# The generator of an S4D kernel: row copies put later, a second PSUM bank for products, doubling factors in one three-bank tile

## The chip, the cores and the metric

The kernel runs on one core of a Trainium2 chip. The metric is the time of one execution on the device in microseconds, as a median over runs. A core has five engines with instruction queues of their own: TensorE (PE, whose weight loads are listed as PEld), VectorE (DVE), ScalarE (ACT), GpSimd (POOL) and SyncE (SP), which here only issues transfers. Engines wait for each other through semaphores.

## The reference

Two sublayers under adaptive layer norm work on a sequence of L = 2048 rows of D = 576 channels. The first is an S4D convolution: a kernel K of 2048 taps is generated for each channel from N = 128 complex modes and convolved causally with the input. The second is a dense feed-forward layer with ReLU and 4608 hidden units.

```python
# convolution
dt = jnp.exp(log_dt)
A = -jnp.exp(log_A_real) + 1j * A_imag
C = (C_real + 1j * C_imag) * dt[:, None]
P = jnp.exp((A * dt[:, None])[:, :, None] * pos[None, None, :])
K = 2.0 * jnp.einsum("dn,dnl->dl", C, P).real
Kf = jnp.fft.rfft(K, L2)
Uf = jnp.fft.rfft(u_t, L2)
y = jnp.fft.irfft(Uf * Kf[None, :, :], L2)[:, :, :L]
...
mod = (_silu(c) @ w_mod).reshape(c.shape[0], 6, 1, -1)
sa, ca, ga, sb, cb, gb = (mod[:, 0], mod[:, 1], mod[:, 2], mod[:, 3], mod[:, 4], mod[:, 5])
h = _layernorm(x, axis=-1) * (1 + ca) + sa
x = x + ga * conv(h)
h = _layernorm(x, axis=-1) * (1 + cb) + sb
x = x + gb * (jnp.maximum(h @ w1, 0) @ w2)
```

## The kernel before

The sequence is cut into four blocks of 512 rows. The convolution's kernel K is generated by the class `KGen` for block 0 first, in its method `first`, while nothing else can run; then `main` runs the convolution of block 0 (`conv(0)`, which starts with the layer norm of its rows x), and from there on the feed-forward layer, with the remaining blocks of K (`rest`) and the remaining convolutions woven between. The change lies in `first` and what it calls.

K at tap 32a + b of a channel is a sum over the modes, which lie on the 128 partitions, of a coarse factor W1 (16 values of a) and a fine factor W2 (32 values of b), both complex. A group g is 96 channels, as two halves u of H = 48; the six groups run in three pairs (`CHUNKS`: groups 0 and 1, 2 and 3, 4 and 5). The text calls them pair 0, 1 and 2. The program of a pair, as it is written:

- `raw(c)` makes the arguments of a pair: 22 "turns" k, each an ACT copy to integers and a DVE subtraction (L105, L115), and 38 exponentials E on ACT. For pair 1 and 2 this code is issued between the groups of the pair before.
- `values(g, then)` makes W2 of group g, first the odd half of its slots, then `then()`, then the even half (`half_values`). ACT takes sines s (into two PSUM banks) and cosines c of the turns; DVE makes the imaginary parts of W2 (L150, L151) and POOL the real ones (helper at L59). POOL also clears and copies one slot of each W2 (L163, L164). `start` makes the products tc (POOL) and Tc (DVE) that open W1. `powers` makes four doubling factors Zp in PSUM, and two more, zs, in SBUF: ACT's sines and cosines, then times E on DVE (L199) and on POOL. W2 and zs are stored to DRAM on SP.
- `make(g)` doubles W1 four times with the factors Zp (`doubling`: DVE multiplies t and T at L224 and L225 and adds at L227 and L228; in the last doubling POOL adds, "W<-T,T" in the profile), stores W1, and runs 384 matmuls on PE (`products`, L236) from W1 and W2 into one PSUM bank, kps. It returns `rows`, which copies kps to rows of K in SBUF on ACT (ke), and with every third group stores them (kd_0_0 and kd_0_1, L323) on SP.

In the loop of `first`, the first group's row copy of a pair stands right after its `make` and one step of the next `raw`; the second group's stands in `then` of the first group of the next pair, between its odd and even half.

ACT and POOL run in program order, as the helpers `act` and `pool` keep it. The order on DVE, PE and SP is set by the scheduler of the language from the program and its dependencies.

Of PSUM's eight banks the sines take two, the temporary T one, the factors Zp four (two tiles of two banks), and kps one. Beside this, `mod` works out three of the modulation vectors (ga, ca, sa) from w_mod on PE; their weights wm_ga, wm_ca, wm_sa are loaded into the first three of the five rotating buffers ("slots") of W2's tag, and their products go through the same bank as kps. One of those products is issued ahead of the values, one in `then` of group 0, one after pair 0's values. W2_n names half n = 2g + u.

With the pools of `KGen` closed, the pool of `conv(0)` lies over the same part of SBUF. Its tile cb of `mod_late` (L524, L525, 160 columns, a copy of ct on DVE) lies over one of W2's slots, and in DVE's queue stands ahead of the layer norm's statistics (BN_STATS, L692).

Of the kernel before, what the change touches and what calls it, by code (L numbers as in the profile page):

```python
# [10 lines left out]
F32 = mybir.dt.float32  # L11
# [7 lines left out]
P = 128  # L19
# [6 lines left out]
G = 96  # L26
# [14 lines left out]
def strips(t, k):  # L41

    w = t.shape[1] // k
    return bass.AP(tensor=t.tensor, offset=t.offset, ap=[[w, P], [P * w, k], [1, w]])


class KGen:
# [10 lines left out]
    def pool(self, out, a, b, op):  # L58
        self.tc.keep_in_program_order(self.nc.gpsimd.tensor_tensor(out, a, b, op=op))  # L59

    def open(self, ctx):

        pool = lambda n, **kw: ctx.enter_context(self.tc.tile_pool(name=n, bufs=1, **kw))
        self.pa, self.pc, self.pt, self.pw = (pool(f"kg_{x}") for x in "actw")
        self.ps, self.ph = pool("kg_ps", space=PSUM), pool("kg_ph", space=PSUM)

    def bank(self, name):
        return self.ph.tile([P, 512], F32, tag="ph", name=name)

    def setup(self, I):  # L70
        nc, pc = self.nc, self.pc
# [115 lines left out]
    def powers(self, g, e, f):  # L187

        v, p = self.nc.vector.tensor_tensor, self.pool
        Z = self.ps.tile([P, 2, 512], F32, tag="Z", bufs=2, name=f"Zp_{g}")[:, :, 0 : 4 * G]  # L190
        Z = Z.rearrange("p r (i c) -> p r i c", c=G)
        zs = self.pc.tile([P, 2, 2, G], F32, tag="zs", bufs=2, name=f"zs_{g}")
        c = self.abs(f)
        self.act(Z[:, 1], f[:, 0:4], AF.Sin, scale=-TWO_PI)
        self.act(zs[:, :, 1], f[:, 4:6], AF.Sin, scale=-TWO_PI)
        self.cos(Z[:, 0], c[:, 0:4])
        self.cos(zs[:, :, 0], c[:, 4:6])
        for r in (1, 0):
            v(Z[:, r], Z[:, r], e[:, 0:4], op=ALU.mult)  # L199
            p(zs[:, :, r], zs[:, :, r], e[:, 4:6], op=ALU.mult)  # L200
        self.Z[g] = Z, zs

    def doubling(self, g):

        v, p = self.nc.vector.tensor_tensor, self.pool
        W1, Z = self.W1[g], self.Z[g][0]
        flat = "p u a r c -> p u (a r) c"
# [22 lines left out]
    def products(self, ps, W1, W2, u):  # L230

        for q in range(12):
            for dd in range(4):
                ch = dd * 12 + q
                for r in range(2):
# [6 lines left out]
                    )  # L242

    def first(self, setup, mod):

        nc, k = self.nc, self.k
        self.W1, self.Z, W2s, EF, ke = {}, {}, {}, {}, {}

        def raw(c):
            w = slice(CHUNKS[c][0] * G, CHUNKS[c][1] * G)  # L250
            F, E = self.turns(w), [None] * 5
            for m in (2, 3, 0, 1, 4):
                E[m] = self.exps(w, m)
                if m in (3, 1):
                    yield
            for g in range(*CHUNKS[c]):
                gs = slice((g - CHUNKS[c][0]) * G, (g - CHUNKS[c][0]) * G + G)
                EF[g] = [e[:, :, gs] for e in E], [f[:, :, gs] for f in F]

        def values(g, then):  # L260
            E, F = EF.pop(g)
            W2 = W2s[g] = [
                self.pw.tile([P, 2, 32, H], F32, tag="W2", bufs=5, name=f"W2_{2 * g + u}")
                for u in range(2)
            ]
            self.half_values(g, W2, E[2:4], F[0], True)
            then()
            self.half_values(g, W2, E[0:2], F[1], False)
            for u in range(2):
                nc.sync.dma_start(  # L270
                    out=strips(k.W2d[2 * g + u], 4),
                    in_=W2[u].rearrange("p r (y b) c -> p (r y) (b c)", y=2),
                )
            self.powers(g, E[4], F[2])
            zs = self.Z[g][1]
            for u in range(2):
                nc.sync.dma_start(out=k.Zd[2 * g + u], in_=zs[:, :, :, u * H : u * H + H])

        def make(g):
            self.doubling(g)  # L280
            for u in range(2):
                nc.sync.dma_start(
                    out=strips(k.W1d[2 * g + u], 2),
                    in_=self.W1[g][:, u].rearrange("p (y a) r c -> p y (a r c)", y=2),
                )
            if g % 3 == 0:
                ke[0] = self.pc.tile([P, 16, 72], F32, tag="ke", bufs=1, name=f"ke_{g}")
            ps = self.bank(f"kps_{g}")[:, :384].rearrange("p (q a) -> p q a", a=16)
            for u in range(2):
                self.products(ps, self.W1[g], W2s[g][u], u)  # L290

            def rows():
                qs = slice(24 * (g % 3), 24 * (g % 3) + 24)
                self.act(ke[0][:, :, qs], ps.rearrange("p q a -> p a q"), AF.Copy)
                if g % 3 == 2:
                    self.store(0, g // 3, ke[0].rearrange("p a q -> p (a q)"), nc.sync)

            return rows

        next(mod)  # L300
        for _ in raw(0):
            pass
        next(mod)
        setup()
        rows = lambda: next(mod)
        for c, (a, b) in enumerate(CHUNKS):
            for g in range(a, b):
                values(g, rows if g == a else lambda: None)
            if c == 0:
                next(mod)  # L310
            later = raw(c + 1) if c + 1 < len(CHUNKS) else iter(())
            next(later, None)
            for g in range(a, b):
                rows = make(g)
                next(later, None)
                if g + 1 < b:
                    rows()
        return rows

    def store(self, s, p, ke, eng):  # L320

# [104 lines left out]
class Body:  # L426
# [41 lines left out]
    def mod(self, kg):  # L468

        nc, I = self.nc, self.I  # L470
        self.ct = ct = self.cst.tile([P, 5], F32, name="ct")
        ex = kg.pc.tile([P, 5], F32, name="ex")
        nc.vector.memset(ct, 0.0)
        nc.sync.dma_start(out=ct[:, 0:4], in_=I["c"][0:512].rearrange("(k p) -> p k", p=P))
        nc.sync.dma_start(out=ct[0:64, 4:5], in_=I["c"][512:576].unsqueeze(1))
        names = (
            (2, "ga", kg.pw, "W2", 5), (1, "ca", kg.pw, "W2", 5), (0, "sa", kg.pw, "W2", 5)
        )
        ws = {}
        for i, nm, pool, tag, bufs in names:  # L480
            w = ws[nm] = pool.tile([P, 5, D], F32, tag=tag, bufs=bufs, name=f"wm_{nm}")
            self.mod_weights(w, slice(i * D, (i + 1) * D), nc.sync)
        yield
        kg.act(ex, ct, AF.Exp, scale=-1.0)
        nc.vector.tensor_scalar(ex, ex, 1.0, None, op0=ALU.add)
        nc.vector.reciprocal(ex, ex)
        nc.vector.tensor_tensor(ct, ct, ex, op=ALU.mult)
        cb = kg.pc.tile([P, 5, P], F32, name="cb")
        self.mod_lhs(cb)
        self.m = {}  # L490
        ga = kg.pc.tile([P, 2, PC], F32, name="m_ga")
        for i, nm, *_ in names:
            t = ga if nm == "ga" else self.cst.tile([P, 2, PC], F32, name=f"m_{nm}")
            for h in range(2):
                ps = kg.bank(f"mps_{nm}")[:, :PC]
                self.mod_product(ps, cb, ws[nm][:, :, h * PC : (h + 1) * PC])
                if nm == "ga":
                    nc.vector.tensor_copy(t[:, h], ps)
                elif nm == "ca":
                    nc.vector.scalar_tensor_tensor(  # L500
                        t[:, h], ps, 1.0, ga[:, h], op0=ALU.add, op1=ALU.mult
                    )
                else:
                    nc.vector.tensor_tensor(t[:, h], ps, ga[:, h], op=ALU.mult)
            self.m[nm] = t.rearrange("p h c -> p (h c)")
            yield
# [685 lines left out]
```

## Time and profile before

| | |
|---|---|
| median of 3 runs | 1453.64 us (1451.17, 1453.64, 1460.19) |
| profiled execution | 1457.43 us, its span 1455.7 us |
| mean granted TensorE clock | 0.925 |
| busy in the span | PE 1241.2 us (85%), PEld 982.0 (67%), DVE 880.0 (60%), ACT 498.0 (34%), POOL 189.3 (13%) |

Busy microseconds of each engine by stage, with the granted clock of TensorE and the mean busy share of the DMA engines. The first four stages are `first` (start and pair 0, pair 1, pair 2, the last products):

| stretch, us | PE | DVE | ACT | POOL | clock | DMA |
|---|---|---|---|---|---|---|
| 0 to 65 | 20.98 | 41.95 | 48.58 | 23.42 | 0.90 | 0.56 |
| 65 to 119 | 13.29 | 39.71 | 32.86 | 26.77 | 0.56 | 0.50 |
| 119 to 162 | 13.69 | 29.49 | 17.82 | 27.07 | 0.54 | 0.58 |
| 162 to 198 | 13.73 | 19.00 | 3.00 | 9.07 | 0.50 | 0.85 |
| 198 to 1455 | 1179.55 | 749.84 | 395.77 | 102.94 | 0.97 | 0.72 |

The profile is one execution. A line of a timeline gives the start of a run of like instructions, the time to the end of the last, engine, line, operation, what is written and read, and how many; a bracket behind it gives the idle time of the engine before it and what ended that.

### The profile page before, as it was taken

To read this page: it belongs to the slowest core of one execution; us is meant where nothing else is said; L and a number is where in the kernel's file an instruction comes from. 1 tells how busy PE (TensorE), PEld (TensorE's weight loads), DVE (VectorE), ACT (ScalarE), POOL (GpSimd) and SP (SyncE) were. 2 spreads that over 40 slices of the span, in tenths; PEclk is the share of its full clock that TensorE was granted. 3 is DMA by queue.
4 is the path that set the end of the run, shared out by engine and by line. 5 is a ranking of instruction groups with operands and counts; after the bars stand their busy time and mean duration, and the time that the engine had idled before them with its cause. 6 is when DMAs were issued, how large, how long until landed. Compare 5 with 4: busy or idle time off the path is not lost. (4 is left out here: it accounts for less than half of the span.)

```text
span 1455.7 us, 25966 instructions
## 1 busy us (share of the span) xinstructions
PE 1241.2 (85%) x10600; PEld 982.0 (67%) x10600; DVE 880.0 (60%) x1355; ACT 498.0 (34%) x1002; POOL 189.3 (13%) x273
## 2 busy tenths in 40 slices
PE   2523267799989997789999999989999999999997
PEld 1323245577867765567787777767887878888885
DVE  4866669799946589756846698444799431111101
ACT  7574231422221241152224322623332353323231
POOL 2463602010021110002110110010100000000000
PEclk9755568899999999989999999999999999999998
DMA  4653968567698774849967999575989656666661
GB/s 150 228 204 130 340 222 274 175 224 250 208 351 322 258 268 167 300 130 371 327 221 274 327 319 325 158 230 163 332 307 362 196 160 204 205 199 196 197 188 58
DMA packets 135110, 346.49 MB, mean 238 GB/s; under 512 B 23440, under 2 KB 23728, under 8 KB 134992
## 3 DMA queue, kind: packets, MB, share of 16 engines
q1 hardware_dynamic: 107008, 218.82, 46.5%
q0 software_dynamic: 27696, 125.43, 23.7%
q8 instruction: 83, 1.36, 0.4%
q10 hardware_dynamic: 288, 0.59, 0.1%
q14 instruction: 35, 0.29, 0.1%
HBM read 261.04 MB, written 83.76 MB: 237 GB/s over the span
## 5 line engine op out<-in xcount | busy, mean ns | idle before, releaser
L1009 PE MATMUL acc<-hh,w 128*128 128x512 f32 x1296 | 421.6, 400 | 3.0 <-DVE w L970 2.6
L984 PE MATMUL hps<-xh,w 128*128 128x512 f32 x1152 | 397.8, 405 | 0.1
L990 DVE SCALAR_TENSOR_TENSOR hl<-hps,hh 128x512 fp32r<-128x512 f32 x144 | 99.0, 687 | 320.7 <-ACT hh L989 320.4
L1009 PE MATMUL acc<-hl,w 128*128 128x512 f32 x720 | 280.9, 401 | 0.1
L1009 PEld LDWEIGHTS acc<-hh,w 128*128 128x128 f32 x1296 | 242.8, 189 | 56.3 <-DVE w L970 3.1
L984 PEld LDWEIGHTS hps<-xh,w 128*128 128x128 f32 x1152 | 218.7, 191 | 47.8 <-ACT xh L916 1.3
L984 PE MATMUL hps<-xl,w 128*128 128x512 f32 x576 | 231.9, 403 | 0.5 <-DVE xl L921 0.5
L989 ACT ACTIVATE hh<-hps 128x512 fp32r<-128x512 f32 x144 | 86.1, 598 | 328.1 <-PE hps L984 325.4
L967 ACT ACTIVATE w<-r 128x576 fp32r<-128x576 f32 x144 | 98.9, 687 | 277.1 <-PE acc L1009 215.0
L1009 PEld LDWEIGHTS acc<-hl,w 128*128 128x128 f32 x720 | 135.9, 189 | 29.4 <-DVE hl L990 0.5
L984 PEld LDWEIGHTS hps<-xl,w 128*128 128x128 f32 x576 | 109.6, 190 | 25.3 <-DVE xl L921 1.9
L236 PE MATMUL kps<-W,W 128*32 128x16 f32 x2304 | 41.0, 219 | 99.4 <-POOL W L59 66.5
L984 PE MATMUL hps<-xs,w 128*128 128x512 f32 x288 | 103.4, 424 | 21.5 <-DVE hl L990 6.9
L958 ACT ACTIVATE w<-r 128x640 fp32r<-128x640 f32 x144 | 105.5, 733 | 38.6 <-DMA L1d<-w 38.6
L236 PEld LDWEIGHTS kps<-W,W 128*32 128x32 f32 x2304 | 38.6, 150 | 102.2 <-POOL W L59 68.3
L382 PEld LDWEIGHTS kps<-W1r,W2r 128*32 128x32 f32 x3456 | 67.9, 146 | 35.9 <-issue 23.7
L382 PE MATMUL kps<-W1r,W2r 128*32 128x48 f32 (+2 forms) x3456 | 76.8, 238 | 12.9 <-issue 8.1
L820 DVE TENSOR_TENSOR Y<-Y,T 128x1152 f32<-128x1152 f32 x64 | 84.7, 1350 | 0.1
L984 PEld LDWEIGHTS hps<-xs,w 128*128 128x128 f32 x288 | 54.4, 192 | 37.7 <-ACT w L958 7.6
L645 ACT ACTIVATE Z<-ps_f 128x288 f32<-128x288 f32 x120 | 48.3, 413 | 69.6 <-PE ps_f L644 63.9
L1110 POOL DMA_DIRECT2D out_dram<-x x16 | 8.8, 550 | 477.4 <-DVE x L1108 477.4
L841 PE MATMUL ps_i<-V,gc 128*128 128x288 f32 x136 | 43.5, 450 | 6.1 <-DVE x L846 4.2
(200 smaller groups left out, 1422.1 us busy)
## 6 DMA issues: line engine op xcount, KB each, us to landing
r<-in_w_dram SPq DMA_DIRECT2D x144, 320.0 KB, 3.8
r<-in_w_dram SPq DMA_DIRECT2D x144, 288.0 KB, 3.9
w<-L1d SPq DMA_DIRECT2D x108, 320.0 KB, 3.0
w<-L2d SPq DMA_DIRECT2D x108, 288.0 KB, 3.4
W2r<-W2d POOLq DMA_DIRECT2D x18, 1536.0 KB, 9.6
W2d<-W SPq DMA_DIRECT2D x12, 1536.0 KB, 6.7
Ua<-Ud POOLq DMA_DIRECT2D x15, 1152.0 KB, 10.9
W<-W1d POOLq DMA_DIRECT2D x18, 768.0 KB, 9.3
```

What stands on the lines that cost most here:

```text
L236: self.nc.tensor.matmul(ps[32 * dd : 32 * dd + 32, 12 * u + q, :], W2[:, r, :, ch], W1[:, u, :, r, ch], start=(r == 0), stop=(r == 1),)
L382: nc.tensor.matmul(ps[32 * dd : 32 * dd + 32, q, :], W2[:, r, :, ch], W1[:, :, r, ch], start=(r == 0), stop=(r == 1),)
L645: ev = nc.scalar.activation(Z[:, n2, c], ps[:, :PC], AF.Copy)
L820: v(y, y, T, op=op or ALU.add)
L841: nc.tensor.matmul(ps[:, :PC], a, b, start=(i == 0), stop=(i == len(ops) - 1))
L958: nc.scalar.activation(w[:, 0], r, AF.Copy)
L967: nc.scalar.activation(w[:, 0:D], r, AF.Copy)
L984: nc.tensor.matmul(ps, a, x, start=(i == 0), stop=(i == 13))
L989: nc.scalar.activation(hh, ps, AF.Relu)
L990: nc.vector.scalar_tensor_tensor(hl, ps, 0.0, hh, op0=ALU.max, op1=ALU.subtract)
L1009: nc.tensor.matmul(acc[i], a, x, start=(f == 0 and j in (0, 3, 6, 9, 12)), stop=(f == NF - 1 and j in (2, 5, 8, 11, 13)),)
L1110: nc.gpsimd.dma_start(out=ov[:, n2], in_=x2[:, n2])
```

## The change

Four things. The row copies: `rows` of a pair's two groups are kept in a list, and issued in the next pair, the first in `then` of its second group (behind that group's odd values and so behind the first group's even sines), the second after it; the tile ke is allocated when it is first written. The product of ca moves with this from `then` of group 0 to that of group 1. The bank: `bank` rotates over two PSUM banks. The factors: all Zp lie in one tile of three banks, group g in its half g % 2, 768 columns to a half; the middle bank holds the end of the one half and the start of the other. The weights of sa go to W1's tag (three buffers) in place of W2's, so that W2_0 takes the third slot in place of the fourth, and every later W2 the slot before its old one.

```diff
@@ open
         self.ps, self.ph = pool("kg_ps", space=PSUM), pool("kg_ph", space=PSUM)
+        self.Zp = self.ps.tile([P, 2, 8 * G], F32, name="Zp")
...
     def bank(self, name):
-        return self.ph.tile([P, 512], F32, tag="ph", name=name)
+        return self.ph.tile([P, 512], F32, tag="ph", bufs=2, name=name)
...
@@ powers
-        Z = self.ps.tile([P, 2, 512], F32, tag="Z", bufs=2, name=f"Zp_{g}")[:, :, 0 : 4 * G]
-        Z = Z.rearrange("p r (i c) -> p r i c", c=G)
+        Z = self.Zp[:, g % 2].rearrange("p (r i c) -> p r i c", r=2, c=G)
...
@@ make
-            if g % 3 == 0:
-                ke[0] = self.pc.tile([P, 16, 72], F32, tag="ke", bufs=1, name=f"ke_{g}")
...
             def rows():
+                if g % 3 == 0:
+                    ke[0] = self.pc.tile([P, 16, 72], F32, tag="ke", bufs=1, name=f"ke_{g}")
...
@@ first
-        rows = lambda: next(mod)
+        rows = [lambda: next(mod), lambda: next(mod)]
         for c, (a, b) in enumerate(CHUNKS):
             for g in range(a, b):
-                values(g, rows if g == a else lambda: None)
-            if c == 0:
-                next(mod)
+                values(g, rows.pop(0) if g > a else lambda: None)
+            rows.pop(0)()
             later = raw(c + 1) if c + 1 < len(CHUNKS) else iter(())
             next(later, None)
             for g in range(a, b):
-                rows = make(g)
+                rows.append(make(g))
                 next(later, None)
-                if g + 1 < b:
-                    rows()
-        return rows
+        rows[0]()
+        return rows[1]
...
@@ mod
-            (2, "ga", kg.pw, "W2", 5), (1, "ca", kg.pw, "W2", 5), (0, "sa", kg.pw, "W2", 5)
+            (2, "ga", kg.pw, "W2", 5), (1, "ca", kg.pw, "W2", 5), (0, "sa", kg.pc, "W1", 3)
```

In the rows below, numbers behind a name count the tiles of the program (k_192_521 is a tile of turns of pair 1, c_1081 the cosines of group 2, c_1142 those of group 3), and differ a little between the two programs; lines of the changed kernel are up to two off.

ACT at the start of pair 1, before: both row copies of pair 0 stand here, one ahead of the last exponentials, one behind the first cosine of group 2.

```order
L56 ACTIVATE E_192_827<-lar_227 128x192 x8
L56 ACTIVATE ke_0_624<-kps_0_625 128x16x24
L56 ACTIVATE E_192_1068<-lar_227 128x192 x6
L56 ACT_TABLE_LOAD
L56 ACTIVATE s_4_1077<-k_192_521 128x384
L56 ACTIVATE s_5_1079<-k_192_521 128x384
L56 ACTIVATE c_1081<-k_192_521 128x768
L56 ACTIVATE c_1081<-c_1081,halfpi_232 128x768
L56 ACTIVATE ke_0_624<-kps_1_875 128x16x24
L56 ACTIVATE c_1101<-k_192_538 128x768
```

The same stretch after:

```order
L56 ACTIVATE E_192_825<-lar_228 128x192 x8
L56 ACTIVATE E_192_1065<-lar_228 128x192 x6
L56 ACT_TABLE_LOAD
L56 ACTIVATE s_4_1074<-k_192_520 128x384
L56 ACTIVATE s_5_1076<-k_192_520 128x384
L56 ACTIVATE c_1078<-k_192_520 128x768
L56 ACTIVATE c_1078<-c_1078,halfpi_233 128x768
L56 ACTIVATE c_1097<-k_192_537 128x768
```

No copy is left in it. The place to which the first copy went, behind the odd cosine of group 3 (ACT, after):

```order
L56 ACTIVATE s_6_1133<-k_192_520 128x384
L56 ACTIVATE s_7_1135<-k_192_520 128x384
L56 ACTIVATE c_1137<-k_192_520 128x768
L56 ACTIVATE c_1137<-c_1137,halfpi_233 128x768
L56 ACTIVATE ke_0_1156<-kps_0_623 128x16x24
L56 ACTIVATE c_1158<-k_192_537 128x768
L56 ACTIVATE s_6_1160<-k_192_537 128x384
```

The copy of kps_1 follows eight instructions further on, behind group 3's factors.

DVE at the end of pair 1's values, before: three rows of the doubling of W1_2 stand ahead of the factors of group 3 and the turns of the next pair.

```order
L151 SCALAR_TENSOR_TENSOR W2_7_1137<-s_7_1165,E_192_818 128x7x48
L224 TENSOR_TENSOR t_1261<-W1_2_1084,Zp_2_1122 128x192
L225 TENSOR_TENSOR T_1262<-W1_2_1084,Zp_2_1122 128x192
L227 TENSOR_TENSOR W1_2_1084<-t_1261,T_1262 128x2x48
L199 TENSOR_TENSOR Zp_3_1182<-Zp_3_1182,E_192_1068 128x384
L115 SCALAR_TENSOR_TENSOR k_384_1196<-th_228,k_384_1196 128x192
L199 TENSOR_TENSOR Zp_3_1182<-Zp_3_1182,E_192_1068 128x384
L115 SCALAR_TENSOR_TENSOR k_384_1196<-th_228,k_384_1196 128x192 x7
L115 SCALAR_TENSOR_TENSOR k_384_1213<-th_228,k_384_1213 128x192 x8
L115 SCALAR_TENSOR_TENSOR k_384_1230<-th_228,k_384_1230 128x192 x6
L228 TENSOR_TENSOR W1_2_1084<-t_1261,T_1262 128x2x48
```

And after:

```order
L152 SCALAR_TENSOR_TENSOR W2_7_1132<-s_7_1162,E_192_816 128x7x48
L199 TENSOR_TENSOR Zp_227<-Zp_227,E_192_1065 128x384 x2
L116 SCALAR_TENSOR_TENSOR k_384_1193<-th_229,k_384_1193 128x192 x8
L116 SCALAR_TENSOR_TENSOR k_384_1210<-th_229,k_384_1210 128x192 x8
L116 SCALAR_TENSOR_TENSOR k_384_1227<-th_229,k_384_1227 128x192 x6
L224 TENSOR_TENSOR t_1258<-W1_2_1081,Zp_227 128x192
L225 TENSOR_TENSOR T_1259<-W1_2_1081,Zp_227 128x192
L227 TENSOR_TENSOR W1_2_1081<-t_1258,T_1259 128x2x48
L228 TENSOR_TENSOR W1_2_1081<-t_1258,T_1259 128x2x48
```

All doubling rows now stand behind both products of the factors and the turns; in pair 0 six such rows move in the same way.

DVE at the start of `conv(0)`, with the semaphores that a row waits for, before: cb waits for the store of W2_10 and for PE (up to the last product that reads W2_10).

```order
L225 TENSOR_TENSOR T1_2130<-W1_5_1822,Zp_5_1859 128x768
L224 TENSOR_TENSOR T0_2135<-W1_5_1822,Zp_5_1859 128x768 [waits DVE_49,Pool_49]
L225 TENSOR_TENSOR T1_2136<-W1_5_1822,Zp_5_1859 128x768
L525 COPY cb_2579<-ct_244 128x160 [waits DMAHW2_49,PE_49]
L692 BN_STATS st1_2377<-x2_0_2371 128x6 [waits DMAHW5_49]
```

And after:

```order
L225 TENSOR_TENSOR T1_2124<-W1_5_1813,Zp_227 128x768
L224 TENSOR_TENSOR T0_2129<-W1_5_1813,Zp_227 128x768 [waits DVE_49,Pool_49]
L225 TENSOR_TENSOR T1_2130<-W1_5_1813,Zp_227 128x768
L523 COPY cb_2574<-ct_245 128x160 [waits DMAHW3_49,PE_49]
L690 BN_STATS st1_2372<-x2_0_2366 128x6 [waits DMAHW5_49]
```

The row stands where it stood; the store that it waits for is now that of W2_11, and the PE product the last one that reads W2_11. On SP, the two stores of kd_0_0 move from between the stores of W1 of groups 2 and 3 to ahead of the store of W2_10, and two loads of Fourier factors (fcU, fcK) move behind the last stores of W1, ahead of the load of x.

## The prediction

> **What bounds the kernel now.** I read the span and the busy time by stage (tabled above) first, then the waits of the stretch that changes, then the engines' timelines there, and last the first instructions of the stage behind it.
>
> ```profile
> span 1455.7 us, 25966 instructions
> ```
>
> From 198 us on PE is busy for 1179.55 of 1257 us. No instruction changes there, so I let that part start earlier or later and keep its length. The change lies ahead of it, where no engine is full. ACT's longest wait in the pairs' middle, and DVE's (74 to 158 us; total, times, longest):
>
> ```profile
> ACT ke L56 <- PE kps L236: 42.0, 4, 15.3
> ...
> DVE W L150 <- ACT s L56: 12.6, 2, 6.4
> ```
>
> ACT stands 42.0 us before row copies that nobody needs soon; its sines are queued behind them, and DVE and POOL starve. What counts is POOL's idle time, because POOL's series of products ends last in each pair and DVE's turns and doublings follow it. POOL in pair 1 (start, length, and in brackets the idle time before):
>
> ```profile
> 73.03 3.90 POOL L59 TENSOR_TENSOR W<-T,T 128x384 f32<-128x384 f32 x4 [5.42 <-DVE T L225]
> 81.99 0.59 POOL L59 TENSOR_TENSOR tc<-cc,c 128x192 f32<-128x192 f32 x1 [5.05 <-ACT c L56]
> ...
> 90.74 3.68 POOL L59 TENSOR_TENSOR W<-c,E 128x384 f32<-128x384 f32 x4 [3.81 <-ACT c L56]
> ...
> 95.77 0.61 POOL L59 TENSOR_TENSOR tc<-cc,c 128x192 f32<-128x192 f32 x1
> 96.32 7.51 POOL L59 TENSOR_TENSOR W<-c,E 128x384 f32<-128x384 f32 x8
> 103.78 1.14 POOL L59 TENSOR_TENSOR zs<-zs,E 128x192 f32<-128x192 f32 x2
> ```
>
> And in pair 2:
>
> ```profile
> 127.43 3.90 POOL L59 TENSOR_TENSOR W<-T,T 128x384 f32<-128x384 f32 x4 [5.42 <-DVE T L225]
> 135.91 0.61 POOL L59 TENSOR_TENSOR tc<-cc,c 128x192 f32<-128x192 f32 x1 [4.58 <-ACT c L56]
> ...
> 144.48 3.68 POOL L59 TENSOR_TENSOR W<-c,E 128x384 f32<-128x384 f32 x4 [3.62 <-ACT c L56]
> ```
>
> **The sum, by pairs.** Gains are positive.
>
> T0, pair 0. Here nothing is copied yet; what goes is POOL's wait for wm_ca, whose W2 slot now falls to the next pair.
>
> ```profile
> 45.86 5.84 POOL L59 TENSOR_TENSOR W<-c,E 128x384 f32<-128x384 f32 x6 [3.57 <-PE mps_ca L519]
> ```
>
> ```profile
> 49.76 5.38 DVE L115 SCALAR_TENSOR_TENSOR k<-th,k 128x192 f32<-128x192 f32 x11
> ```
>
> ```profile
> 98.52 0.34 DVE L224 TENSOR_TENSOR t<-W,Zp 128x192 f32<-128x192 f32 x1
> 98.78 0.35 DVE L225 TENSOR_TENSOR T<-W,Zp 128x192 f32<-128x192 f32 x1
> 99.17 0.25 DVE L227 TENSOR_TENSOR W<-t,T 128x96 f32<-128x96 f32 x1
> 99.41 0.57 DVE L199 TENSOR_TENSOR Zp<-Zp,E 128x384 f32<-128x384 f32 x1
> 100.04 5.10 DVE L115 SCALAR_TENSOR_TENSOR k<-th,k 128x192 f32<-128x192 f32 x1
> 105.06 0.55 DVE L199 TENSOR_TENSOR Zp<-Zp,E 128x384 f32<-128x384 f32 x1
> 105.53 5.72 DVE L115 SCALAR_TENSOR_TENSOR k<-th,k 128x192 f32<-128x192 f32 x21
> ```
>
> Beside POOL a turn k took 5.38/11 = 0.49 us, alone 5.72/21 = 0.27; eleven lose 2.4 us, and POOL's end comes at most 3.57 us earlier. Against that, six doubling rows (t, T, W, W, t, T), which filled DVE's waits, move behind the k's; by the rows from 98.52 to 99.41 a t, a T and a W are 0.9 us, so six rows, two of them of twice the size, are some 2.2 us, an estimate. The gain lies between 2.4 − 2.2 = +0.2 and 3.57 − 2.2 = +1.4. I take +0.5, nearer the low end, since the k's are bound by DVE there.
>
> T1, pair 1. The two row copies leave ACT's queue ahead of the sines, so POOL's 5.05 + 3.81 = 8.86 us go; POOL then runs gap-free from 76.93. But POOL's clearing of W2_8, ahead of tc of group 3, waits for the last product that reads W2_3, which is kps_1's end, and that wait can now come last:
>
> ```profile
> 76.53 0.86 PE L236 MATMUL kps<-W,W 128*32 128x16 f32 x32 [0.67 <-ACT ke L56]
> ```
>
> ```profile
> 87.80 0.49 ACT L56 ACTIVATE ke<-kps 128x384 f32<-128x384 f32 x1 [5.95 <-PE kps L236]
> ```
>
> The copy at 87.80 started as kps_1 ended. With a second bank kps_1 needn't wait 0.67 us for kps_0's copy, so it ends at about 87.1, and tc follows at 87.3 in place of 95.77: 8.5 us. The gain lies between 8.5 and 8.86; I take +8.5. The copies themselves (0.49 us each) now stand behind the second group's odd cosine and behind its factors, when POOL has over 8 us of work ahead of it, and hide there.
>
> T2, pair 1. The shared middle bank moves the three rows t, T, W at the pair's end behind the k's: −0.9, as the k at 100.04 had to wait for POOL's end (104.92) anyway and the rows were free ahead of it. In exchange the second Zp (105.06 to 105.53) comes ahead of that k: +0.5. Net −0.5; if the k's slip in, nothing.
>
> T3, pair 2. POOL's 4.58 + 3.62 = 8.20 go. DVE's rows t, T, W again move behind both Zp, which before overlapped ACT's factors: 0 to −0.9, I take −0.3. So +7.9; the products of group 4 start 0.5 + 8.5 − 0.5 + 7.9 = 16.4 us earlier, near 145.5.
>
> The tail, on PE and on DVE:
>
> ```profile
> 161.94 0.29 PE L236 MATMUL kps<-W,W 128*32 128x16 f32 x2 [20.44 <-POOL W L59]
> ...
> 177.64 0.79 PE L236 MATMUL kps<-W,W 128*32 128x16 f32 x26 [0.67 <-ACT ke L56]
> ...
> 191.36 1.82 PE L236 MATMUL kps<-W,W 128*32 128x16 f32 x103 [1.45 <-issue]
> 198.22 2.29 PE L644 MATMUL ps_f<-kt,fcK 128*128 128x288 f32 x4 [5.04 <-DVE kt L758]
> ```
>
> ```profile
> 188.69 0.32 DVE L525 COPY cb<-ct 128x160 f32<-128x160 f32 x1 [16.82 <-PE kps L236]
> ```
>
> T4. The second bank also lets kps_5 start without ke_4's copy: +0.67, the gap at 177.64 (at least 0, at most that gap).
>
> T5. DVE's copy cb, which stands ahead of the layer norm's statistics, waits for the product that last read the slot below it. Before that was W2_10's, done at 188.69, with another 191.36 + 1.82 = 193.18 to kps_5's end. With slots shifted by one it is W2_11's, the last of all: 193.18 − 188.69 = −4.5. Behind cb stand the layer norm and all of the next stage on DVE, so this is lost in full, unless x lands later still. It landed by 188.69 before; its load is queued on SP behind the stores of W1 that move with the chain, so it lands by 172.3, plus the two factor loads moved ahead of it. cb comes at 193.18 − 16.4 − 0.7 = 176.1. I put it at nothing, with some 3 us left.
>
> Smaller moves: kd_0_0's stores now stand ahead of W2_10's store on SP, and wait only for ke_2's copy, well before; the allocation of ke in rows() and the sa weights in W1's tag release nothing that anybody waits for. Nothing, either way within 0.5 us, covered by SP's idle queue.
>
> Sum: 0.5 + 8.5 − 0.5 + 7.9 + 0.7 − 4.5 = 12.6 us. The profiled execution took 1457.43 us (span 1455.7), so 1444.8; the median of the runs lies 3.8 lower, so 1441.0, or −0.87%.
>
> **Two rules weighed.** The wait in the row at 100.04 came with POOL busy. The Trainium skill, "SBUF — State Buffer", section "Who interferes with whom", says that VectorE's second port pair is shared with GpSimd under an exclusive lock; held per instruction, it would let a k in at each boundary between two of POOL's instructions. The rows at 49.76 agree, the row at 100.04 doesn't. By that rule 1 to 1.5 us more would be gained, an estimate. The reordering of the doubling rows has its reason in "PSUM — Partial Sum Buffer", section "PSUM bank collisions raise a hardware error", of the Trainium skill: two engines must not touch one bank in the same partitions at once, so ACT's factor writes and DVE's doubling reads of the shared bank must be put in order. No run here shows a collision.
>
> **Rivals.**
> R1, more is gained: the k's slip between POOL's instructions as at 49.76 (T2 and T0 at their good ends, +1.4), and the last pair's products get shorter. kps_4 ran from 161.94 to 177.64 − 0.67 = 176.97, 15.0 us, kps_1 from 76.53 to 87.80, 11.3; if an earlier start leaves half of that excess in two groups behind, +3. Gain 17.0: 1436.6. For it: the DMA engines were busy 0.85 of 162 to 198 us. Against: the stores move along with the products.
>
> R2, less: kps_0 and kps_1, now beside a busier ACT and POOL, stretch as kps_4 did, in the gaps that the profile puts down to issue, 3.8 us each, and POOL's clearing of W2_8, now behind kps_1's end, passes all of it on. Gain 12.6 − 7.6 = 5.0: 1448.6. Against it, the DMA engines' share around them was low (the last three numbers are the granted clock, the DMA engines' share and GB/s):
>
> ```profile
> 60.00:90.00 30.00, 13.54 (x768) 12.74 (x768) 17.74 (x40) 8.71 (x20) 12.77 (x17) 0.61 0.29 108
> ```
>
> R3, slower: reading the factors from the one tile, whose halves cross bank borders, costs DVE more. Its doublings' factor reads:
>
> ```profile
> L225 DVE TENSOR_TENSOR T<-W,Zp 128x384 f32<-128x384 f32 (+2 forms) x36 | 23.5, 654 | 0.2
> ...
> L224 DVE TENSOR_TENSOR t<-W,Zp 128x384 f32<-128x384 f32 (+1 forms) x24 | 12.0, 500 | 0.4
> ...
> L224 DVE TENSOR_TENSOR T<-W,Zp 128x768 f32<-128x768 f32 x12 | 11.4, 947 | 0.0
> ```
>
> That is 46.9 us, nearly all on the chain. From +27% the gain is gone; from +58% (12.6 + 14.5) it is slower by over 1%; at double it gives 1441.0 + 47 = 1488. Nothing in the trace shows a read that crosses banks; L224's 947 ns for 768 elements are less than twice the 500 for mostly 384, so a read costs by its elements, and a fixed extra on one border would be small.
>
> **How the numbers follow.** The sum with its own bounds 0.60 (T0 0.2 to 1.4, T1 up to 8.9, T3 7.3 to 8.2, T2 at best 0, x late by up to 3: 1439 to 1445); R1 0.22, R2 0.13, R3 0.05. The range 1435 to 1449 takes in the sum's own, R1 and R2, and leaves R3 out. About 1%, 14.5 us, is what a measurement of this kernel can tell from no change: faster means below 1439.1. That is R1, and the low edge of the sum with the scatter of the runs (1451.17 to 1460.19 before): 0.22 + 0.10 = 0.32; slower is R3, 0.05; within 1% the rest, 0.63.
>
> **What would show it.** ACT's waits of ke on kps fall from 42.0 us to under 6 in the middle; POOL shows no idle time ahead of tc in pair 1 and W2_8's clearing starts at kps_1's end (T1); the three rows stand behind the k's, one k still takes about 5 us (T2); group 4's products start near 145.5 (T3); no gap on PE between kps_4 and kps_5 (T4); cb starts at kps_5's end, and ps_f<-kt near 186 (T5). Wrong it is if kps_1 ends late (R2), if the rows of L224 and L225 get longer (R3), if cb waits for x, or if PE's time behind 198 us changes.

## The result

The changed kernel took 1442.02 us (median of 5 runs, 1439.74 to 1443.16) where the kernel before took 1453.64 (1450.35 to 1460.19). The ratio is 0.9917, with a 95% interval of 0.9888 to 0.9945. Forecast were 1441.0 us and a change within 1%.

The page's span and, of the waits between 74 and 146 us of the changed kernel, ACT's two longest (total, times, longest):

```profile
span 1440.7 us, 25957 instructions
```

```profile
ACT s L56 <- DVE W L152: 22.3, 4, 10.8
...
ACT ke L56 <- DMA kd<-ke: 7.2, 1, 7.2
```

The 42.0 us before row copies are gone. ACT now waits for a free bank for its sines, which means that it runs ahead of DVE. The 7.2 us stand before the copy of kps_3, which goes to a new tile ke while the old one is still being stored; they hold nothing up, as only the next copy stands behind it in ACT's queue. POOL's timeline in pair 1 (start, length, idle time before in brackets):

```profile
72.27 3.92 POOL L59 TENSOR_TENSOR W<-T,T 128x384 f32<-128x384 f32 x4 [5.42 <-DVE T L225]
76.13 0.60 POOL L59 TENSOR_TENSOR tc<-cc,c 128x192 f32<-128x192 f32 x1
...
87.49 0.14 POOL L165 MEMSET W<- 128x48 f32 x1 [1.36 <-issue]
87.63 0.59 POOL L59 TENSOR_TENSOR tc<-cc,c 128x192 f32<-128x192 f32 x1
88.18 7.97 POOL L59 TENSOR_TENSOR W<-c,E 128x384 f32<-128x384 f32 x8
96.11 1.36 POOL L59 TENSOR_TENSOR zs<-zs,E 128x192 f32<-128x192 f32 x2
```

Both waits for ACT's cosines are gone. What is left is 1.36 us before the clearing of W2_8, which begins just after the last product of kps_1 (85.70 + 1.68 = 87.38, below). DVE and PE of the same profile:

```profile
88.25 0.42 DVE L158 TENSOR_TENSOR W<-tc,Tc 128x96 f32<-128x96 f32 x2 [4.67 <-POOL tc L59]
...
91.42 10.30 DVE L116 SCALAR_TENSOR_TENSOR k<-th,k 128x192 f32<-128x192 f32 x22
101.64 0.34 DVE L224 TENSOR_TENSOR t<-W,Zp 128x192 f32<-128x192 f32 x1
...
176.43 0.32 DVE L523 COPY cb<-ct 128x160 f32<-128x160 f32 x1 [20.98 <-PE kps L236]
176.67 2.96 DVE L690 BATCH_NORM_STATS2 st<-x 128x6 f32<-128x288 f32 x8
```

```profile
85.70 1.68 PE L236 MATMUL kps<-W,W 128*32 128x16 f32 x96 [1.76 <-issue]
...
145.52 0.30 PE L236 MATMUL kps<-W,W 128*32 128x16 f32 x2 [13.03 <-POOL W L59]
...
174.52 1.87 PE L236 MATMUL kps<-W,W 128*32 128x16 f32 x102 [4.16 <-issue]
185.96 4.37 PE L642 MATMUL ps_f<-kt,fcK 128*128 128x288 f32 x10 [9.57 <-DVE kt L756]
```

DVE, which waited for ACT, now waits for POOL (4.67 us at 88.25). Group 4's products start at 145.52, forecast near 145.5. cb starts as kps_5 ends (174.52 + 1.87 = 176.39), and the next stage's first product stands at 185.96 in place of 198.22: 12.26 us earlier.

The experiments are read by four such marks, which repeat more closely than times do. In the table, "products" is the start of group 4's, "statistics" the start of the layer norm's on DVE, "kt" the first product on kt (K as `conv(0)` reads it back), "FFN" the first product of the feed-forward layer (hps), all from the profiled executions; each ratio is to the kernel before on the same chip.

| kernel | ratio to before (95%) | products | statistics | kt | FFN |
|---|---|---|---|---|---|
| before | 1 | 161.94 | 188.93 | 198.22 | 271.00 |
| changed | 0.9917 (0.9888 to 0.9945) | 145.52 | 176.67 | 185.96 | 256.66 |
| e7, changed again | 0.9907 (0.9888 to 0.9927) | 145.37 | 176.51 | 185.81 | 257.88 |
| e12, changed again | 0.9924 (0.9896 to 0.9951) | 144.11 | 175.27 | 184.56 | 256.33 |
| e1, sa in W2's tag | 0.9883 (0.9856 to 0.9909) | 145.51 | 171.99 | 181.30 | 252.65 |
| e11, e1 again | 0.9877 (0.9853 to 0.9901) | 146.23 | 172.81 | 182.12 | 252.93 |
| e2, cb apart | 0.9890 (0.9869 to 0.9911) | 145.39 | 171.58 | 180.90 | 253.28 |
| e3, one bank | 0.9958 (0.9940 to 0.9977) | 153.63 | 182.91 | 192.21 | 263.59 |
| e4, early copies | 1.0002 (0.9984 to 1.0021) | 162.46 | 191.96 | 201.26 | 272.64 |
| e5, before with one tile | 1.0007 (0.9989 to 1.0025) | 166.30 | 191.93 | 201.23 | 271.85 |
| e6, slots on ACT | 0.9918 (0.9891 to 0.9945) | 144.50 | 174.59 | 183.88 | 255.79 |
| e8, x on ACT | 0.9888 (0.9865 to 0.9912) | 149.96 | 145.66 | 178.18 | 252.33 |
| e9, statistics behind | 0.9897 (0.9865 to 0.9930) | 144.57 | 154.42 | 177.01 | 250.11 |
| e10, e9 and slots on ACT | 0.9864 (0.9834 to 0.9894) | 144.41 | 154.25 | 175.40 | 248.82 |

The changed kernel's three profiles show how far marks repeat: within 1.4 us ahead of the feed-forward layer, and 1.6 at its start. Beside it only e1 has a second profile (e11, within 0.8 us ahead of that layer), so a smaller difference between two rows isn't shown by them.

### The profile page after: what moved, and what is told of

Its sections match the earlier page's. It is cut to its first block, busy times and chain, and to the rows that moved or that the text cites. A ratio compares the mean times of both kernels' runs of the same rounds, so it can differ in the third digit from the quotient of the medians.

```text
span 1440.7 us, 25957 instructions
## 1 busy us (share of the span) xinstructions
PE 1239.4 (86%) x10600; PEld 982.6 (68%) x10600; DVE 880.7 (61%) x1355; ACT 498.3 (35%) x1002; POOL 189.3 (13%) x273
## 3 DMA queue, kind: packets, MB, share of 16 engines
q8 instruction: 83, 1.36, 0.4%
## 5 line engine op out<-in xcount | busy, mean ns | idle before, releaser
L642 PE MATMUL ps_f<-kt,fcK 128*128 128x288 f32 x112 | 39.8, 449 | 13.6 <-DVE kt L756 9.6
## 6 DMA issues: line engine op xcount, KB each, us to landing
Ua<-Ud POOLq DMA_DIRECT2D x15, 1152.0 KB, 11.6
```

The source lines that it names most:

```text
L642: nc.tensor.matmul(o, fc[:, n2, c, :], src(n2), start=True, stop=True)
```

## The experiments

**e4: the copies back where they were.** Two banks, the one factor tile and the new slots stay.

```diff
-                values(g, rows.pop(0) if g > a else lambda: None)
-            rows.pop(0)()
+                if c == 0:
+                    values(g, (lambda: next(mod)) if g > a else lambda: None)
+                else:
+                    values(g, rows if g == a else lambda: None)
...
-                rows.append(make(g))
+                rows = make(g)
                 next(later, None)
+                if g + 1 < b:
+                    rows()
```

> The changed kernel with the row copies where they were before the change, two banks and the one factor tile kept. Theory: ACT waits some 40 us for kps again, POOL idles 8.5 and 8.2 us in pairs 1 and 2 again, group 4's products start near 161.5, cb still waits for kps_5's end, time 1458. Rival (the second bank or the new slots carry the gain, and not the copies' place): time 1442 to 1446.

The median was 1457.79 us. The waits between 74 and 158 us of this kernel:

```profile
ACT ke L56 <- PE kps L236: 43.8, 4, 17.0
```

Group 4's products start at 162.46 and the ratio to before is 1.0002: without the copies' new place, bank, tile and slots together gain nothing. The copies' place alone doesn't carry it either, as the next run shows.

**e3: one bank, the copies late.**

```diff
-        return self.ph.tile([P, 512], F32, tag="ph", bufs=2, name=name)
+        return self.ph.tile([P, 512], F32, tag="ph", bufs=1, name=name)
```

> The changed kernel with one bank for products, the copies as late as changed. Theory: kps_1 starts only after ke_0's copy in group 3's values (near 83.5), ends near 95, POOL's clearing of W2_8 and tc of group 3 wait for it (near 95.2 in place of 87.63), in pair 2 W2_11 waits for the first half of kps_3 (+3.5), the tail pays 0.7 again: group 4's products near 156.6, time 1453.8. Rival (the second bank is worth only the gaps of 0.67 us that the copies left): time 1443.3, group 4's products near 146.

The median was 1448.69 us. The size lies between theory and rival, and the way wasn't the one expected: tc of group 3 came at 88.24, since in this kernel's order the clearing of W2_8 no longer stands ahead of it. PE and DVE of e3:

```profile
51.66 5.06 PE L517 MATMUL mps_sa<-wm_sa,cb 128*128 128x288 f32 x10 [4.15 <-DVE m_sa L502]
```

```profile
56.75 0.46 DVE L502 TENSOR_TENSOR m_sa<-mps_sa,m_ga 128x288 f32<-128x288 f32 x1 [2.20 <-PE mps_sa L517]
...
93.06 0.56 DVE L151 TENSOR_TENSOR W<-s,E 128x384 f32<-128x384 f32 x1 [2.90 <-PE kps L236]
...
100.37 6.00 DVE L116 SCALAR_TENSOR_TENSOR k<-th,k 128x192 f32<-128x192 f32 x22 [4.34 <-ACT k L56]
```

With one bank the second half of sa's product waits 4.15 us for DVE's read of the first, and DVE then 2.20 us for it, with two of pair 1's turns and all of pair 0's doublings behind; POOL's first adds come at 65.42, 2.5 us after the changed kernel's 62.95. POOL's wait for mps_ca is gone here too, by the slots. In pair 1 kps_1 runs late, DVE waits 2.90 us for it, and ACT's second copy holds up the integer copies of the turns (4.34 us). The second bank is worth 8.1 us at group 4's products and 6.2 at the statistics, about half of the gain. The copies' new place without the one tile was not run.

**e5: the kernel before with the one tile alone.**

```diff
+        self.Zp = self.ps.tile([P, 2, 8 * G], F32, name="Zp")
...
-        Z = self.ps.tile([P, 2, 512], F32, tag="Z", bufs=2, name=f"Zp_{g}")[:, :, 0 : 4 * G]
-        Z = Z.rearrange("p r (i c) -> p r i c", c=G)
+        Z = self.Zp[:, g % 2].rearrange("p (r i c) -> p r i c", r=2, c=G)
```

> The kernel before with one part of the change alone: all factors in the one three-bank tile, copies, bank and slots as before. Theory (the shared middle bank only moves doubling rows behind the factors and the turns): pair 0 ends 0.5 to 2.2 us later, pair 1 another 0.5, pair 2 0.3; group 4's products near 164 (161.94 before), cb near 190.7 (188.69), time 2 us over before. A read of the factors costs what it did (L224 and L225 500, 654 and 947 ns). Rival (reads that cross a bank cost more): those rows get longer, by 12 us and more in all.

The median was 1456.53 us, beside 1456.41 for the kernel before on the same chip. The factor reads of e5 (busy, mean ns, idle before):

```profile
L225 DVE TENSOR_TENSOR T<-W,Zp 128x384 f32<-128x384 f32 (+2 forms) x36 | 23.5, 654 | 0.2
...
L224 DVE TENSOR_TENSOR t<-W,Zp 128x384 f32<-128x384 f32 (+1 forms) x24 | 12.0, 501 | 0.4
...
L224 DVE TENSOR_TENSOR T<-W,Zp 128x768 f32<-128x768 f32 x12 | 11.4, 948 | 0.0
```

The means are those of before (654, 500 and 947 ns). By the tile's layout only six of these 72 reads cross a border, all among the rows of 384 elements, whose means (558 ns at L225, 552 at L224) were 558 and 551; of the twelve products of factors and E on DVE six cross, and their mean stays 562 ns. So crossing costs nothing that shows here, and R3 falls. The moved rows do cost, more than expected (group 4's products at 166.30, near 164 expected). POOL's first adds come at 65.59 in place of 63.70, 1.9 us; from tc of group 3 to the next pair's adds 23.13 us (96.42 to 119.55) in place of 22.33, 0.8; from tc of group 5 to group 4's products 13.74 (152.56 to 166.30) in place of 12.50, 1.2. At the statistics 3.0 us are left, at the feed-forward layer 0.85, and the times don't tell that from nothing.

**e1 and e11: sa back in W2's tag.** ca's product goes back to group 0's values, as that slot order needs.

```diff
-(1, "ca", kg.pw, "W2", 5), (0, "sa", kg.pc, "W1", 3)
+(1, "ca", kg.pw, "W2", 5), (0, "sa", kg.pw, "W2", 5)
...
-        rows = [lambda: next(mod), lambda: next(mod)]
+        rows = [lambda: next(mod), lambda: None, lambda: next(mod)]
...
-                values(g, rows.pop(0) if g > a else lambda: None)
+                values(g, rows.pop(0) if g > a or g == 0 else lambda: None)
```

> The changed kernel with the weights of sa back in W2's tag and ca's product back in group 0's values, all else as changed. Theory (the shifted slots cost 4.5 us at the end and gain 0.8 in pair 0): POOL's wait for mps_ca returns and group 4's products start near 146.3 (145.52 in the changed kernel); cb waits only for the first half of kps_5, so it comes before 173 and the statistics start when x has landed, near 173 in place of 176.67. Time 1438.4. Rival a (the end is bound by something else than cb): the statistics near 177, time 1442.8. Rival b (POOL's wait of 3.57 us is paid in full): group 4's products near 149, statistics near 176, time 1441.5.

> e1 once more (sa's weights in W2's tag), beside the changed kernel on one chip: its statistics start 4.7 us earlier, so 0.3% below the changed kernel; the rival (the gain is lost behind) gives the same time.

The medians were 1439.45 and 1436.36 us. DVE of e1, and POOL and PE in its pair 0:

```profile
168.94 0.32 DVE L523 COPY cb<-ct 128x160 f32<-128x160 f32 x1 [13.51 <-PE kps L236]
171.99 2.98 DVE L690 BATCH_NORM_STATS2 st<-x 128x6 f32<-128x288 f32 x8 [2.73 <-DMA x<-in_x_dram]
```

```profile
44.30 3.71 POOL L59 TENSOR_TENSOR W<-c,E 128x384 f32<-128x384 f32 x4
47.94 1.17 POOL L59 TENSOR_TENSOR zs<-zs,E 128x192 f32<-128x192 f32 x2
...
63.46 2.94 POOL L59 TENSOR_TENSOR W<-T,T 128x384 f32<-128x384 f32 x3 [5.06 <-DVE T L225]
```

```profile
36.01 5.70 PE L517 MATMUL mps_ca<-wm_ca,cb 128*128 128x288 f32 x20
```

The price of the shifted slots is as forecast: cb leaves the path, and the statistics start 4.7 us earlier, now on x. But POOL's wait for mps_ca does not come back. With two banks ca's 20 matmuls run in one piece and end at 41.71; before, the second ten started at 41.25 and took 4.53 us. So the bank alone removes this wait, as the slots alone do in e3. The shifted slots are worth 0.5 us in pair 0 (63.46 and 62.95), and group 4's products start no earlier by them. Beside the changed kernel on one chip the ratios to before are 0.9877 and 0.9924; the intervals overlap by a hair (0.9901 and 0.9896), but all six runs of e11 (1434.71 to 1438.37 us) lie below all six of the changed kernel (1439.79 to 1447.53).

**e2: cb in the pool of constants.**

```diff
-        cb = self.cv.tile([P, 5, 32], F32, name="cb")
+        cb = self.cst.tile([P, 5, 32], F32, name="cb")
```

> The changed kernel with cb in the pool of constants, where it lies over no W2 slot and is copied early. Theory: the statistics start when x has landed, near 172.3 in place of 176.67, and everything behind moves with it: first product on kt near 181.6 (185.96 now), time 1437.7. Rival (the next stage is bound by kps_5 in another way, through PE's queue or the second half of K's rows): the statistics start early, but the first product or the inverse transforms do not, time 1442.

The median was 1439.75 us. DVE of e2:

```profile
171.58 2.98 DVE L690 BATCH_NORM_STATS2 st<-x 128x6 f32<-128x288 f32 x8 [16.26 <-DMA x<-in_x_dram]
```

The same 5 us by another edit: what mattered was cb's wait. Of 5.1 us at the first product on kt, 3.4 reach the feed-forward layer (256.66 to 253.28).

**e6: W2's single slots written by ACT.**

```diff
-                nc.gpsimd.tensor_copy(W2[u][:, 0, 23], El[:, 7, uc])
-                nc.gpsimd.memset(W2[u][:, 1, 23], 0.0)
+                self.act(W2[u][:, 0, 23], El[:, 7, uc], AF.Copy)
+                self.act(W2[u][:, 1, 23], El[:, 7, uc], AF.Copy, scale=0.0)
```

> The changed kernel with the single slot of each W2 (a copy of E and a zero) written by ACT in program order, in place of POOL. Theory (POOL's series is the bound, and its clearing of W2_8 waits for kps_1): tc of group 3 comes 2.2 us earlier, pair 2 gains 0.7 more, group 4's products start near 142.6 (145.52), cb near 173.5 (176.43), time 1439.1. Rival (POOL's series isn't the bound, or ACT's extra writes are): group 4's products near 145.5, time 1442.

The median was 1443.03 us. POOL and DVE of e6 in pair 1:

```profile
85.54 0.58 POOL L59 TENSOR_TENSOR tc<-cc,c 128x192 f32<-128x192 f32 x1
86.08 7.56 POOL L59 TENSOR_TENSOR W<-c,E 128x384 f32<-128x384 f32 x8
93.61 1.13 POOL L59 TENSOR_TENSOR zs<-zs,E 128x192 f32<-128x192 f32 x2
```

```profile
90.36 10.25 DVE L116 SCALAR_TENSOR_TENSOR k<-th,k 128x192 f32<-128x192 f32 x22
```

Beside the changed kernel's first profile tc comes 2.1 us earlier, as expected, and POOL ends 2.7 us earlier (94.74 for 97.47), but the turns end only 1.1 us earlier (100.61 for 101.72): they now stood still until POOL was done. Group 4's products come 1.0 us earlier, which is within what a repeat moves (e12, unaltered, has tc at 86.20, its turns done at 100.29 and the products at 144.11), and the time shows nothing. POOL's series is not the bound by itself: when the turns get to run counts too.

**e8, e9 and e10: x earlier.** With cb gone the statistics wait for x, whose load is queued on SP behind the stores of W1. e8 has e2's and e6's edits and issues this load on ACT's queue.

```diff
-        (nc.gpsimd if s else nc.sync).dma_start(
+        (nc.gpsimd if s else nc.scalar).dma_start(
             out=x2, in_=self.I["x"][s].rearrange("n m d -> m n d")
```

> The changed kernel with cb in the pool of constants, W2's single slots written by ACT, and the load of x issued on ACT's queue behind group 5's factors, so that it lands near 148. Theory (with cb gone x is what the stage waits for, and behind it PE's products of groups 4 and 5): the statistics are done among the last doublings, and the first product on kt follows the end of kps_5, near 175 (185.96 in the changed kernel); time 1431. Rival (the layer norm, some 9 us of DVE, now delays the doublings of the last pair and with them kps_5): the first product near 181, time 1437.

The median was 1440.65 us. DVE of e8:

```profile
145.66 0.46 DVE L690 BATCH_NORM_STATS2 st<-x 128x6 f32<-128x288 f32 x1 [5.10 <-DMA x<-in_x_dram]
```

The rival held in part, by another way: the scheduler put the first of the statistics among the doublings, where DVE stood 5.10 us for x, and group 4's products started at 149.96. e9 keeps the statistics behind the last doubling, by the helper that keeps program order (on those two kinds of instruction), and leaves the slots on POOL; e10 adds e6's edit.

```diff
-                v(T.rearrange(flat), X[:, u], zi[:, u], op=ALU.mult)
+                last = v(T.rearrange(flat), X[:, u], zi[:, u], op=ALU.mult)
+                if m == 8:
+                    self.tc.keep_in_program_order(last)
...
-            self.nc.vector.bn_stats(out=st[i], in_=src(i))
+            bs = self.nc.vector.bn_stats(out=st[i], in_=src(i))
+            if kept:
+                self.tc.keep_in_program_order(bs)
```

> The changed kernel with cb in the pool of constants, the load of x on ACT's queue behind group 5's factors, and the layer norm's statistics kept behind the last doubling on DVE (W2's single slots on POOL, as changed). Theory (8's loss came from statistics that stood among the doublings and waited 5.1 us for x): group 4's products near 145.4, statistics near 155.5, first product on kt right behind kps_5, near 176.5 (185.96 in the changed kernel, 178.2 in e8), time 1435. Rival (from here on what the stage waits for lies behind the first product, in ACT's evictions and the second half of K's rows): first product near 177, but the feed-forward layer's first product no earlier than in e8 (252.3), time 1439.

> As e9, and W2's single slots written by ACT. Theory: another 1.0 to 1.9 us, as e6 showed in its rows (group 4's products near 144.4, first product on kt near 175.5), time 1433.5. Rival (with the slots on ACT the turns wait for the whole of POOL's series, as in e6): no gain over e9.

The medians were 1438.62 and 1433.75 us. e9's marks came within 1.1 us of its theory, but its time near the rival's 1439; e10's marks and time came as its theory had them. DVE and PE of e10:

```profile
154.25 2.97 DVE L692 BATCH_NORM_STATS2 st<-x 128x6 f32<-128x288 f32 x8
```

```profile
175.40 5.62 PE L644 MATMUL ps_f<-kt,fcK 128*128 128x288 f32 x16
...
190.00 5.17 PE L644 MATMUL ps_f<-h,fcU 128*128 128x288 f32 x10 [3.65 <-ACT Z L645]
...
227.40 3.85 PE L536 MATMUL mps_gb<-wm_gb,cb 128*32 128x128 f32 x50 [5.28 <-DMA wm_gb<-in_w_mod_dram]
```

The first product on kt now follows kps_5 without a gap. Of 9.2 us gained there against e12, 7.5 reach the feed-forward layer (256.33 to 248.82); ACT's evictions (3.65 us) and the load of wm_gb (5.28 us) are late next. By its interval e10 beats the changed kernel on the same chip (0.9834 to 0.9894 against 0.9896 to 0.9951), and the kernel before. That e10 beats e9 isn't shown: the intervals overlap, and group 4's products start alike.

**e7 and e12: the changed kernel again.**

> The changed kernel once more, unaltered, beside the others on one chip: ratio to before 0.9917 as measured first (its interval 0.9888 to 0.9945).

> The changed kernel, unaltered, as the mark for the other three on this chip: ratio to before near 0.991.

The medians were 1442.26 and 1442.27 us.

## Why the prediction was right

Time, range and sign came as forecast. By terms, with the gains measured at the same marks:

| term | forecast | measured | from |
|---|---|---|---|
| T0, pair 0 | +0.5 | +0.75 | POOL's first adds, 63.70 to 62.95 |
| T1, pair 1 | +8.5 | +7.4 | tc of group 3, 95.77 to 87.63, less T0 |
| T2, moved rows | −0.5 | +0.6 | the next adds, 118.10 to 109.39, less T0 and T1 |
| T3, pair 2 | +7.9 | +7.7 | group 4's products, 161.94 to 145.52, less those |
| T4, second bank | +0.7 | +0.4 | start of kps_4 to end of kps_5, 31.24 to 30.87; cause not shown |
| T5, cb's wait | −4.5 | −4.5 | cb 4.49 ahead of kps_5's end before, 0.04 behind it now |
| sum at cb | 12.6 | 12.3 | 188.69 to 176.43 |

The changed kernel's other two profiles (e7, e12) give the same terms within 0.4 us, but for T1, which is 7.2 and 8.8.

T1 and T3, which are nearly everything, rest on the copies' place, and e4 shows that: with the copies back, the ratio is 1.0002. They need the second bank beside it: with one bank (e3) group 4's products gain 8.3 us of 16.4. T1 fell short by 1.1 us because kps_1 ended at 87.38 and not at 86.35 (87.1 less the measured T0). The time lies in gaps that the profile puts down to issue, as R2 had it, but nothing ties it to a busier ACT and POOL: in e12 kps_1 ends at 85.94, the clearing of W2_8 does not wait, and T1 comes near its upper bound of 8.86.

T4's gap of 0.67 us is gone from PE, but the 0.4 us can't be put down to it: e3, which pays the gap, takes 29.01 us for the same two groups, and over all runs they take 28.29 us (e8) to 32.51 (e9). What sets this length, mostly gaps put down to issue, stays open. T5 is shown by e1 and e2, which win 4.7 and 5.1 us back at the statistics.

The part behind, whose length the prediction kept, took 1257.5 us from the first product on kt to the end before, and 1254.8, 1255.3 and 1253.5 in the changed kernel's profiles, with PE busy for 1179.55 us before and 1174.22 to 1180.54 after. With one profile of the kernel before, and medians 11.6 us apart (12.3 at cb), this is not shown to be a gain.

The step in T0 that named its cause failed, and that its size held is luck. The prediction let POOL's wait for ca's product go by the shifted slots, and gave 2.4 to 3.57 us for it. The slots do remove the wait (e3), but with one bank and the moved rows that brings POOL's first adds only from 65.59 (e5) to 65.42 (e3): the turns then stand for sa's product. The second bank, which the prediction did not count in pair 0, gives the other 2.5 us (65.42 to 62.95); without the shifted slots it gives 2.1 (65.59 to 63.46 in e1). The moved rows cost 1.9 (e5), near the estimate of 2.2.

T2 was mis-sized in both directions (its own two terms, −0.9 and +0.5, make −0.4). The moved rows cost 0.8 us in pair 1 and 1.2 in pair 2 (e5), more than forecast. But in the changed kernel the turns slipped between POOL's instructions, which was the first half of R1. Its second half did not come: the last two groups' products took 30.87 us after 31.24. That T1 came 1.1 us too low and T2 1.1 too high is why the sum is so close: that, too, is luck.

## What to carry to other kernels

An instruction that only empties a result belongs behind the work that other engines wait for in the same queue, and it needs a second buffer, or its lateness comes back through the producer (e3 lost half of the gain). When buffers of a rotating tag shift, ask which of them lies under the next stage's first tile: a small copy behind the last reader cost 4.5 us. A gain at a mark in the middle is not a gain at the end: of 9 us at one stage's first product some 7.5 reached the next stage.

## What the runs showed of the hardware

A turn on DVE beside a series of products on POOL has two courses. In pair 1 of the kernel before, e5, e6, e8, e9 and e10 the first turn stands until POOL is done (5.10 us at 100.04 before) and POOL's eight products take 7.5 to 7.6 us. In pair 1 of the changed kernel, e1, e2, e4 and the repeats the turns go in between, about one to a product (none takes more than 1.16 us), and the eight take 7.96 to 7.99 us. The two kernels that were profiled more than once (the changed one and e1) showed the same course each time. In pair 0 it is the other way round: the kernel before lets its turns in (none over 1.18 us), and in the changed kernel one takes 4.19 us.

The Trainium skill, "SBUF — State Buffer", section "Who interferes with whom", has VectorE and GpSimd share a port pair under an exclusive lock. The course in which the turns go in between agrees with a lock held for one instruction, the other does not. What decides between them is open, and no run was made for it alone. The order of the rows and their distance do not settle it: in e9 the first turn came 3.40 us after the start of POOL's eight products and stood, in e12 3.38 us after it and went in between, with the same rows around them.
